# A two-layer SiLU block on one core: transposing two more blocks of x by DMA, and opening with two blocks and eight weight tiles

## The chip, the cores and the metric

The kernel runs on one core of a Trainium2 chip. The metric is the time of one execution on the device in microseconds (us), lower is better. It is given as the median of several runs, with the lowest and highest. The profile is of one execution; its span is about 1.5 us shorter than the time of the same execution. All points in time below are counted from the start of the span. A run is called fast or slow by its granted TensorE clock and its time; a difference under 2% is called "same".

## The reference

```python
B, S, D, F = 1, 2048, 640, 1728          # x [S,D], w1 [D,F], w2 [F,D], all bf16
h = jnp.einsum("bsd,df->bsf", x, w1)
h = silu(h)
out = jnp.einsum("bsf,fd->bsd", h, w2)
```

The first product needs x with its 640 columns on the partitions, so x must be transposed. The words used below:

- A **block** is 128 rows of x (16 of them). A **chunk** is four blocks, 512 rows. Chunk 0 is blocks 0 to 3.
- A **row block** k of w1 is its rows 128k to 128k+127 (five of them, k = 0 to 4). A **tile** ft is 128 columns of w1 (13 of them, and 64 columns left over).
- The **opening pass** is the part in which TensorE works through the row blocks in the order in which they land, and keeps the sums of several tiles open in PSUM, the memory into which TensorE writes.

## The kernel before

All loads are issued by SyncE (`sp`), in the order in which they are needed. The chunks 1 to 3 come transposed by DMA, behind all of w1. The four blocks of chunk 0 are loaded plainly and turned by TensorE.

```python
FA = 6
FG = [(6, 10), (10, FT)]
ld_x[0] = load(sp, x0[:, 0, :], x_v[:, 0, :])
ld_x[1] = load(sp, x0[:, 1, :], x_v[:, 1, :])
FH = 3
ld_k0a = load(sp, w1s[:, 0, 0:FH * P], w1_v[:, 0, 0:FH * P])
for k in range(DT):                       # row blocks of tiles 0 to 5
    lo = FH if k == 0 else 0
    ld_k.append(load(sp, w1s[:, k, lo * P:FA * P], w1_v[:, k, lo * P:FA * P]))
    if k in (1, 2):
        ld_x[k + 1] = load(sp, x0[:, k + 1, :], x_v[:, k + 1, :])
for a, b in FG:                           # tiles 6 to 9, then 10 to the end
    e = F if b == FT else b * P
    pt = load(sp, w1s[:, :, a * P:e], w1_v[:, :, a * P:e])
    ...
for c in range(1, NSC):                   # chunks 1 to 3, transposed by DMA
    for dt in range(DT):
        ld_xc[c] = tick(sp.dma_start_transpose(out=xT[:, dt, c * SCH:(c + 1) * SCH],
            in_=xf[c * SCH:(c + 1) * SCH, dt * P:(dt + 1) * P]), s, 16)
# ... w2 behind them
```

`turn(j, ...)` turns block j with five PE transposes into PSUM, and VectorE and ScalarE copy the result. The opening pass has four blocks and six tiles:

```python
k_pass(0, 0, 1, first=True, fts=range(FH)); ...   # blocks 0 and 1, row block 0
wait(pe, ld_k[1]);  k_pass(1, 0, 2)
t2 = turn(2, 7, 6)
wait(pe, ld_k[2]);  k_pass(2, 0, 2)
wait(pe, *t2)
for k in range(3):
    k_pass(k, 2, 3)                       # block 2 catches up
t3 = turn(3, 7, 6)
wait(pe, ld_k[3]);  k_pass(3, 0, 3)
wait(pe, *t3)
for k in range(4):
    k_pass(k, 3, 4)                       # block 3 catches up
wait(pe, ld_k[4]);  k_pass(4, 0, 4, last=True)
# then tiles 6 to 12 with all 512 columns of chunk 0, then chunks 1 to 3, then the second product
```

## Time and profile before

| | kernel before |
|---|---|
| time | 126.85 us (126.74 to 126.95, 3 runs) |
| TensorE busy | 122.8 of 125.1 us |
| TensorE waits for w1 | none |
| last Silu of chunk 0 starts | 19.82 us |

From the page of the kernel before, busy time and share of the span by engine (PE: TensorE's matmuls, PEld: its weight loads, DVE: VectorE, ACT: ScalarE, POOL: GpSimd; SP is SyncE, L207 is line 207 of the kernel):

```profile
PE 122.8 (98%) x652; PEld 59.0 (47%) x652; DVE 9.0 (7%) x16; ACT 39.9 (32%) x70; POOL 0.8 (1%) x7
```

From the waits of the kernel before (who waited <- for whom: us in total, times, longest), the entries of TensorE that have to do with data; there is none for w1:

```profile
PEld ps L207 <- DVE xT L183: 0.4, 2, 0.2
PEld ps L180 <- DMA x<-in_x_dram: 0.4, 1, 0.4
```

The chain of waits of the kernel before, in order of time from the opening pass on (start, length, what):

```profile
3.87 2.47 PE ps L207 x18
6.34 0.28 PE ps L180 x5
6.62 1.72 PE ps L207 x24
8.34 0.28 PE ps L180 x5
8.62 114.60 PE ps L207 x579
```

The two pieces of 0.28 us are the turns of blocks 2 and 3.

The DMA in that stretch, by microseconds (window and length, then busy time of each engine, granted clock, mean DMA share, GB/s):

```profile
7.00:8.00 1.00, 1.00 (x18) 0.86 (x16) 0.01 (x1) 0.03 (x1) 0.00 (x0) 1.00 0.91 304
8.00:9.00 1.00, 1.00 (x16) 0.81 (x13) 0.34 (x1) 0.34 (x1) 0.00 (x0) 1.00 0.93 309
9.00:10.00 1.00, 1.00 (x15) 0.81 (x14) 0.01 (x1) 0.03 (x1) 0.00 (x0) 1.00 1.06 353
```

Issues of the last two parts of w1 (KB, us from issue to landing):

```profile
w1s<-in_w_dram SPq DMA_DIRECT2D x1, 640.0 KB, 6.5
w1s<-in_w_dram SPq DMA_DIRECT2D x1, 560.0 KB, 7.6
```

They wait in the queue for long, and that harms nothing: the landing records put them at 11.3 and 12.9 us, and TensorE needs them at 12.0 and 16.3 us.

### The profile page before, as it was taken

To read this page: it belongs to the slowest core of one execution; us is meant where nothing else is said; L and a number is where in the kernel's file an instruction comes from. 1 tells how busy PE (TensorE), PEld (TensorE's weight loads), DVE (VectorE), ACT (ScalarE), POOL (GpSimd) and SP (SyncE) were. 2 spreads that over 40 slices of the span, in tenths; PEclk is the share of its full clock that TensorE was granted. 3 is DMA by queue.
4 is the path that set the end of the run, shared out by engine and by line. 5 is a ranking of instruction groups with operands and counts; after the bars stand their busy time and mean duration, and the time that the engine had idled before them with its cause. 6 is when DMAs were issued, how large, how long until landed. Compare 5 with 4: busy or idle time off the path is not lost.

```text
span 125.1 us, 1496 instructions
## 1 busy us (share of the span) xinstructions
PE 122.8 (98%) x652; PEld 59.0 (47%) x652; DVE 9.0 (7%) x16; ACT 39.9 (32%) x70; POOL 0.8 (1%) x7
## 2 busy tenths in 40 slices
PE   8999999999999999999999999999999999999993
PEld 6786444444444444444444443444444443444452
DVE  0220000000000000000000004202020210112021
ACT  4224955555555555555530003010101011010100
POOL 2000000000000000000000000000000000000000
PEclk9999999999999999999999999999999999999999
DMA  5899954446970000000000001441111111111112
GB/s 154 261 313 229 124 125 93 110 100 130 368 280 2 0 0 3 0 0 5 0 0 0 0 0 35 91 147 58 52 52 52 52 52 52 52 58 52 52 56 101
DMA packets 17398, 10.37 MB, mean 83 GB/s; under 512 B 10864, under 2 KB 17392, under 8 KB 17392
## 3 DMA queue, kind: packets, MB, share of 16 engines
q1 hardware_dynamic: 17248, 10.21, 31.2%
q8 instruction: 5, 0.08, 0.3%
q10 hardware_dynamic: 144, 0.07, 0.2%
q14 instruction: 1, 0.01, 0.0%
HBM read 5.16 MB, written 2.62 MB: 62 GB/s over the span
## 4 chain that ended last, share of the span: by engine, by line
PE 98%; ACT 0%; issue 0%; DVEq 0%
PE ps L207 95%; PE ps L171 2%; PE ps L180 1%; ACT o_sb L295 0%; DVEq L403 0%
## 5 line engine op out<-in xcount | busy, mean ns | idle before, releaser
L207 PE MATMUL ps<-xT,w1s 128*128 128x512 bf16 (+4 forms) x328 | 60.1, 353 | 0.0
L207 PE MATMUL ps<-w2s,hT 128*128 128x512 bf16 (+2 forms) x221 | 45.4, 367 | 0.0
L207 PEld LDWEIGHTS ps<-xT,w1s 128*128 128x128 bf16 (+1 forms) x328 | 29.5, 101 | 30.1 <-DVE xT L183 0.4
L211 ACT ACTIVATE hT<-ps 128x512 bf16<-128x512 f32 x52 | 30.3, 602 | 23.2 <-PE ps L207 23.2
L207 PEld LDWEIGHTS ps<-w2s,hT 128*128 128x128 bf16 x221 | 20.9, 98 | 24.5 <-issue 1.1
L295 ACT CAST o_sb<-ps 128x512 bf16<-128x512 f32 (+1 forms) x8 | 4.4, 545 | 42.2 <-PE ps L207 42.2
L207 PE MATMUL ps<-hT,w2s 128*128 128x512 bf16 x52 | 11.4, 379 | 0.0
L293 DVE CAST o_sb<-ps 128x512 bf16<-128x512 f32 (+1 forms) x9 | 6.1, 677 | 39.9 <-PE ps L207 39.9
L207 PEld LDWEIGHTS ps<-hT,w2s 128*128 128x128 bf16 x52 | 5.0, 98 | 6.3 <-issue 0.4
L293 DVE CAST oT<-ps 128x512 bf16<-128x512 f32 x2 | 1.3, 686 | 66.8 <-PE ps L207 66.8
L295 ACT CAST oT<-ps 128x512 bf16<-128x512 f32 x2 | 1.1, 588 | 11.1 <-PE ps L207 11.1
L191 ACT COPY xT<-ps 128x256 bf16<-128x256 bf16 x4 | 1.5, 372 | 5.3 <-PE ps L180 5.3
L171 PE MATMUL ps<-z 128*128 128x256 bf16 x10 | 2.5, 415 | 0.4 <-DVE z L124 0.4
L207 PE MATMUL ps<-w2t,hTt 64*128 64x512 bf16 (+2 forms) x17 | 2.2, 366 | 0.0
L180 PE MATMUL ps<-ident,x 128*128 128x128 bf16 x20 | 2.1, 264 | 0.0
L183 DVE COPY xT<-ps 128x384 bf16<-128x384 bf16 x4 | 1.4, 358 | 7.2 <-PE ps L180 7.2
L180 PEld LDWEIGHTS ps<-ident,x 128*128 128x128 bf16 x20 | 1.7, 119 | 0.4 <-DMA x<-in_x_dram 0.4
L171 PEld LDWEIGHTS ps<-z 128*128 128x128 bf16 x10 | 1.3, 140 | 0.9 <-DVE z L124 0.4
L211 ACT ACTIVATE hTt<-ps 128x512 bf16<-128x512 f32 x2 | 1.2, 597 | 1.1 <-PE ps L207 1.1
L150 ACT ACT_TABLE_LOAD x1 | 1.3, 1283 | 0.7 <-PEq L403 0.7
L207 PEld LDWEIGHTS ps<-w2t,hTt 64*128 64x128 bf16 x17 | 0.7, 94 | 1.4 <-issue 0.8
L207 PE MATMUL ps<-hTt,w2t 64*128 64x512 bf16 x4 | 0.6, 382 | 0.0
(10 smaller groups left out, 1.5 us busy)
## 6 DMA issues: line engine op xcount, KB each, us to landing
out_dram<-o_sb SPq DMA_DIRECT2D x15, 160.0 KB, 1.8
w2s<-in_w_dram SPq DMA_DIRECT2D x1, 1120.0 KB, 6.6
w2s<-in_w_dram SPq DMA_DIRECT2D x1, 960.0 KB, 8.8
w1s<-in_w_dram SPq DMA_DIRECT2D x4, 192.0 KB, 3.6
x<-in_x_dram SPq DMA_DIRECT2D x4, 160.0 KB, 2.5
w1s<-in_w_dram SPq DMA_DIRECT2D x1, 640.0 KB, 6.5
w1s<-in_w_dram SPq DMA_DIRECT2D x1, 560.0 KB, 7.6
xT<-in_x_dram SPq DMA_TRANSPOSE x15, 3.4
```

The source lines that it names most:

```text
L150: act.activation(out=warm[:, :], in_=warm[:, :], func=ACT.Silu)
L171: pe.matmul(ps[:, 3, 0:HB], lhsT=z[:, 0:P], rhs=z[:, :], start=True, stop=True)
L180: ins = pe.transpose(dst, x0[:, j, dt * P:(dt + 1) * P], ident[:, :])
L183: r = tick(dve.tensor_copy(out=xT[:, 0:nv, j * P:(j + 1) * P], in_=v[:, 0:nv * P].rearrange("p (k s) -> p k s", s=P),), s_dve)
L191: r = tick(act.copy(out=xT[:, nv:DT, j * P:(j + 1) * P], in_=a[:, 0:(DT - nv) * P].rearrange("p (k s) -> p k s", s=P),), s_act)
L207: return pe.matmul(o, lhsT=l, rhs=r, start=start, stop=stop, skip_group_check=shared)
L211: r = tick(act.activation(out=out_ap, in_=in_ap, func=ACT.Silu), s_act)
L293: r = tick(dve.tensor_copy(out=out_ap, in_=in_ap), s_dve)
L295: r = tick(act.copy(out=out_ap, in_=in_ap), s_act)
```

## The change

Its intent: the ten PE transposes of blocks 2 and 3 and their copies go away, the opening pass has a plain order, and SyncE gets to its transposes sooner because ScalarE (`act`) issues the rest of w1. The core of the diff:

```diff
-        FA = 6
-        FG = [(6, 10), (10, FT)]
+        FA = 8
+        FG = [(8, 11), (11, FT)]
@@ loads on SyncE @@
-            if k in (1, 2):
-                ld_x[k + 1] = load(sp, x0[:, k + 1, :], x_v[:, k + 1, :])
-        for a, b in FG:
-            ...
-            pt = load(sp, w1s[:, :, a * P:e], w1_v[:, :, a * P:e])
@@ transposes on SyncE: blocks 2 and 3 (256 rows) first @@
-        for c in range(1, NSC):
+        for c in range(NSC):
             s = sem(f"s_xc{c}")
+            t0_, t1_ = (HB if c == 0 else c * SCH), (c + 1) * SCH
             for dt in range(DT):
                 ld_xc[c] = tick(sp.dma_start_transpose(
-                    out=xT[:, dt, c * SCH:(c + 1) * SCH],
-                    in_=xf[c * SCH:(c + 1) * SCH, dt * P:(dt + 1) * P],
+                    out=xT[:, dt, t0_:t1_], in_=xf[t0_:t1_, dt * P:(dt + 1) * P],
                 ), s, 16)
@@ the rest of w1 on ScalarE @@
+        wait(act, ld_k[2])
+        for a, b in FG:
+            e = F if b == FT else b * P
+            pt = load(act, w1s[:, :, a * P:e], w1_v[:, :, a * P:e])
@@ opening: two blocks, eight tiles, two tiles to a PSUM bank @@
-        ... (turns of blocks 2 and 3, catching up)
+        for k in range(1, DT):
+            wait(pe, ld_k[k])
+            k_pass(k, 0, 2)
@@ chunk 0 in halves of 256 columns @@
+        for ft, m in [(8, 2), (10, 1), (11, 2)]:
+            wait(pe, ld_w1[ft])
+            half(ft, m, 0)
+        wait(pe, ld_xc[0])
+        for ft in range(0, FT, 2):
+            half(ft, min(2, FT - ft), HB)
```

More of the change, by code (lines that the diff above doesn't have):

```diff
@@ L132, in bass_standalone__dense_activation_silu__prompt_kernel @@
             ld_k.append(load(sp, w1s[:, k, lo * P:FA * P], w1_v[:, k, lo * P:FA * P]))
-            if k in (1, 2):
-                ld_x[k + 1] = load(sp, x0[:, k + 1, :], x_v[:, k + 1, :])
-        for a, b in FG:
-            e = F if b == FT else b * P
-            pt = load(sp, w1s[:, :, a * P:e], w1_v[:, :, a * P:e])
-            for ft in range(a, b):
-                ld_w1[ft] = pt
         barrier_wait_here(ET.SP)
@@ L213, in silu, with k_pass @@
             return r
-        def k_pass(k, j0, j1, first=False, last=False, fts=range(FA)):
+        wait(act, ld_k[2])
+        for a, b in FG:
+            e = F if b == FT else b * P
+            pt = load(act, w1s[:, :, a * P:e], w1_v[:, :, a * P:e])
+            for ft in range(a, b):
+                ld_w1[ft] = pt
+        def k_pass(k, j0, j1, first=False, fts=range(FA)):
             for ft in fts:
-                if first:
-                    wait(pe, bank_free[ft])
+                bk = ft // 2
+                h = (ft % 2) * HB
+                if first and ft % 2 == 0:
+                    wait(pe, bank_free[bk])
                 ins = mm(
-                    ps[:, ft, j0 * P:j1 * P],
+                    ps[:, bk, h + j0 * P:h + j1 * P],
                     w1s[:, k, ft * P:(ft + 1) * P],
                     xT[:, k, j0 * P:j1 * P],
-                    start=first, stop=(k == DT - 1), shared=True,
+                    start=(first and ft % 2 == 0), stop=(k == DT - 1), shared=True,
                 )
-                if last:
-                    silu(hT[:, ft, 0:SCH], ps[:, ft, :], ft, tick(ins, s_pe))
+                if k == DT - 1 and ft % 2 == 1:
+                    silu(
+                        hT[:, ft - 1:ft + 1, 0:HB],
+                        ps[:, bk, :].rearrange("p (m s) -> p m s", m=2),
+                        bk, tick(ins, s_pe),
+                    )
         wait(pe, *t0, ld_k0a)
@@ L234, in bass_standalone__dense_activation_silu__prompt_kernel @@
         k_pass(0, 1, 2, fts=range(FH, FA))
-        wait(pe, ld_k[1])
-        k_pass(1, 0, 2)
-        t2 = turn(2, 7, 6)
-        wait(pe, ld_k[2])
-        k_pass(2, 0, 2)
-        wait(pe, *t2)
-        for k in range(3):
-            k_pass(k, 2, 3)
-        t3 = turn(3, 7, 6)
-        wait(pe, ld_k[3])
-        k_pass(3, 0, 3)
-        wait(pe, *t3)
-        for k in range(4):
-            k_pass(k, 3, 4)
-        wait(pe, ld_k[4])
-        k_pass(4, 0, 4, last=True)
-        nxt = [FA]
+        for k in range(1, DT):
+            wait(pe, ld_k[k])
+            k_pass(k, 0, 2)
+        nxt = [FA // 2]
         def bank():
@@ L258, in bank, with half @@
             return b
-        for ft in range(FA, FT):
-            wait(pe, ld_w1[ft])
-            b = bank()
-            for k in range(DT):
-                ins = mm(ps[:, b, :], w1s[:, k, ft * P:(ft + 1) * P], xT[:, k, 0:SCH],
-                         start=(k == 0), stop=(k == DT - 1))
-            silu(hT[:, ft, 0:SCH], ps[:, b, :], b, tick(ins, s_pe))
+        def half(ft, m, c0):
+            b = bank()
+            for i in range(m):
+                for k in range(DT):
+                    ins = mm(
+                        ps[:, b, i * HB:(i + 1) * HB],
+                        w1s[:, k, (ft + i) * P:(ft + i + 1) * P],
+                        xT[:, k, c0:c0 + HB],
+                        start=(k == 0 and i == 0), stop=(k == DT - 1), shared=True,
+                    )
+            t = tick(ins, s_pe)
+            silu(hT[:, ft:ft + m, c0:c0 + HB],
+                 ps[:, b, 0:m * HB].rearrange("p (m s) -> p m s", m=m), b, t)
+        for ft, m in [(8, 2), (10, 1), (11, 2)]:
+            wait(pe, ld_w1[ft])
+            half(ft, m, 0)
+        wait(pe, ld_xc[0])
+        for ft in range(0, FT, 2):
+            half(ft, min(2, FT - ft), HB)
         for c in range(1, NSC):
```

## The prediction

> **What bounds it now.** TensorE. In the table of busy time its matmuls cover 122.8 of 125.1 us (98%), and the chain of waits is TensorE for 98% of the span, at full granted clock. The waits view shows TensorE idle some 0.4 us each for the zeroed tile, the first x block and the first xT copy; none for w1 or the transposed blocks. So only less TensorE work, or new idle time, can move the time.
>
> **What goes.** Ten PE transposes: the timeline has them in two groups of five, issued every 56 ns, 0.28 us a group: -0.56 us on the critical path. Their four copies (0.36 to 0.37 us) and two x loads (160 KB each) were hidden.
>
> **What is added to TensorE.** Next to nothing. Starts in the timeline lie 56 ns apart for 128 columns, 109.5 for 256, 162.5 for 384, 216 for 512; weight loads stay hidden, so a split costs about 2.5 ns. Chunk 0 goes from about 113 matmuls to about 138: +0.06 us. One more Silu (0.6 us) falls on an ACT that waits for PE anyway. TensorE: -0.5 us in all.
>
> **What moves.** The old opening had four blocks of work for six tiles of w1: tiles 6 to 9 landed at 11.2 us and were needed at 12.0; the rest landed at 12.8, needed at 16.3. The new opening has half the columns per tile, so it eats w1 about twice as fast: by the spacings, the five k passes end near 9.2 us, tiles 8 to 10 are needed then, tiles 11 and 12 near 10.9, and the DMA-transposed half of chunk 0 near 12.0. But the bytes to move by then are the same (2.87 MB: x and transposes 0.66, w1 2.21), which took until 12.8 us, and ScalarE issues its two loads only when row block 2 of w1 has landed, about 6.2 us (estimate from the landings before), so their data starts near 7 us.
> The DMA table shows x and w1 moving at 230 to 360 GB/s, but 80 to 280 where transposes met the last w1 load (10.5 to 12 us): transpose packets that normally take 18 ns took 1 to 2 us, until the slowest engine had finished its other load. Now this overlap is built in. The Trainium skill, "DMA: Bandwidth & Descriptors", section "Issuing engines are not separate DMA queues", says DMAs from different issuers run on the same 16 DMA engines and interleave, and that a second issuer saves only issue time; the trace shows issue at 0.47 us a load, so ScalarE saves little.
> Estimate: tiles 8 to 10 land at 9.5 to 10.5, 11 and 12 at 11 to 12.5, the transposed half at 12 to 14.5 us. TensorE therefore waits 0.5 to 2.5 us in total between 8 and 14 us. Blocks 4 to 7 are needed near 20 us and should land at 17 to 19.5; the rest is early enough.
>
> **Sum.** 126.85 - 0.5 + about 1.3 = 127.6 us; range 126.2 to 129.4. Chances: faster by over 2%: 0.01; within 2%: 0.90; slower by over 2%: 0.09.
>
> **What would show it.** Right: a new wait of TensorE for w1 or for xT from DMA between 8 and 14 us, 0.5 to 2.5 us; spacing of 256-column matmuls 109 to 110 ns; from 20 us on the two timelines are the same, shifted. Wrong: no such wait (then about 126.3 us); wider spacing of 256-column matmuls; or a wait for blocks 4 to 7.
>
> **What would make it wrong.** If the queues share well and the transposes run ahead of w1, the gain of 0.5 us shows. If transposes hold the engines back for longer than before, or a stall of several us drops TensorE's clock (its matmuls ran at half rate until 5.8 us), it is slower by over 2%.

## The result, and the profile after

The kernel after takes 127.66 us (127.30 to 127.77, 6 runs) against 126.87 us (126.73 to 127.45, 6 runs). The ratio is 1.0053, with a 95% interval of 1.0029 to 1.0076: slower by half a percent, within the 2% that count as the same. Ratios in this document are the mean time of one kernel's fast runs over that of the other's fast runs of the same rounds, so they are not quite the ratio of the quoted medians.

From the page of the kernel after, busy time by engine:

```profile
PE 121.5 (96%) x667; PEld 61.7 (49%) x667; DVE 8.3 (7%) x14; ACT 39.6 (31%) x69; POOL 0.8 (1%) x7
```

TensorE has 1.3 us less busy time in a span that is 1.1 us longer. From the waits of the kernel after, the entries that are new:

```profile
PEld ps L200 <- DMA w1s<-in_w_dram: 2.8, 3, 2.0
PE ps L200 <- DMA w1s<-in_w_dram: 2.4, 4, 1.7
```

Weight loads and matmuls waited for the same landings, so the two lines are to be read together, not added. The chain of waits of the kernel after, in order of time (only its end; SyncE's issues come before):

```profile
2.41 3.68 DMA w1s<-in_w_dram
6.09 0.02 issue
6.11 4.74 DMA w1s<-in_w_dram
10.85 0.05 issue
10.90 113.43 PE ps L200 x598
```

This chain is the whole story of the opening. SyncE's load of row block 2, issued at 2.41 us, lands at 6.09 us; only this releases ScalarE, which issues the load of tiles 8 to 10 at 6.11 us; that lands at 10.85 us, and only then does TensorE go on, without a break to the end. From the timeline of the kernel after:

```profile
4.58 0.56 PEld L200 LDWEIGHTS ps<-xT,w1s 128*128 128x128 bf16 x10 [0.41 <-DMA w1s<-in_w_dram]
5.54 3.39 PEld L200 LDWEIGHTS ps<-xT,w1s 128*128 128x128 bf16 x32 [0.40 <-DMA w1s<-in_w_dram]
6.11 1.14 ACTq L89 DMA_DIRECT2D w1s<-in_w_dram  x2
10.90 11.02 PEld L200 LDWEIGHTS ps<-xT,w1s 128*128 128x128 bf16 x97 [1.97 <-DMA w1s<-in_w_dram]
```

There are waits of 0.4 us for row blocks 0 and 1 (up to 4.58 and 5.54 us) and one of 1.97 us for tiles 8 to 10. The DMA by microseconds:

```profile
7.00:8.00 1.00, 1.00 (x12) 0.90 (x10) 0.00 (x0) 0.00 (x0) 0.00 (x0) 1.00 0.84 141
8.00:9.00 1.00, 1.00 (x12) 0.83 (x9) 0.00 (x0) 0.41 (x1) 0.00 (x0) 1.00 1.00 319
9.00:10.00 1.00, 0.21 (x2) 0.00 (x0) 0.00 (x0) 1.00 (x3) 0.00 (x0) 1.00 1.24 231
```

Between 7 and 8 us the rate falls to 141 GB/s, where the kernel before moved 304. SyncE's row blocks are through (the last landed at 7.47 us), and ScalarE's load, issued at 6.11 us, has its first packet at 7.4 us and its full rate only after 8 us. The engines were not idle in that microsecond (busy share 0.84): about half of the bytes were those of the first transposes, in small packets of 256 B. After 9 us the load is slowed a second time; e5 below comes back to that. The issues of ScalarE's loads:

```profile
w1s<-in_w_dram ACTq DMA_DIRECT2D x1, 480.0 KB, 4.7
w1s<-in_w_dram ACTq DMA_DIRECT2D x1, 400.0 KB, 5.7
```

**The account.** From the last Silu of chunk 0 to TensorE's end there are 103.4 us in both traces (19.82 to 123.20 and 20.94 to 124.32). So the whole difference of the two profiled runs, 1.12 us, arises in chunk 0. It splits as follows; each figure is a sum of distances between matmul starts in the two traces:

| term | us |
|---|---|
| two turns fewer (0.28 each), 25 matmuls more (2.5 ns each) | -0.50 |
| gaps beyond the usual spacing, from the first matmul of the opening pass (3.8 us) on: 0.23 before, 2.72 after | +2.49 |
| half-rate clock after 3.8 us: 0.91 before, 0 after | -0.91 |
| sum | +1.08 |
| measured | +1.12 |

The third term needs a word. At the start TensorE ran at half its rate: 213 ns from start to start for 256 columns, and later 109. In the profiled run of before this lasted until 5.8 us, in that of after until 3.1 us. The Trainium skill, "TensorE: Matmul & The Clock Gate", Part 1, says that the array starts at half rate, is released after a busy window of about 3.4 us, and that the window runs freely, so that the moment varies from run to run. These traces agree in the rates and in the variation; the spread here is larger than the 500 ns named there (3.1 to 6.5 us over the traces).

### The profile page after: what moved, and what is told of

It reads as the page before. It is cut to its first block, busy times and chain, and to the rows that moved or that the text cites. A ratio compares the mean times of both kernels' runs of the same rounds, so it can differ in the third digit from the quotient of the medians.

```text
span 126.2 us, 1523 instructions
## 1 busy us (share of the span) xinstructions
PE 121.5 (96%) x667; PEld 61.7 (49%) x667; DVE 8.3 (7%) x14; ACT 39.6 (31%) x69; POOL 0.8 (1%) x7
## 4 chain that ended last, share of the span: by engine, by line
PE 90%; DMA 7%; SPq 2%; issue 0%; ACT 0%
PE ps L200 90%; DMA w1s<-in_w_dram 7%; SPq L89 2%; ACT o_sb L301 0%; SPq L409 0%
## 5 line engine op out<-in xcount | busy, mean ns | idle before, releaser
L200 PE MATMUL ps<-xT,w1s 128*128 128x512 bf16 (+3 forms) x353 | 59.3, 335 | 2.4 <-DMA w1s<-in_w_dram 2.4
L200 PEld LDWEIGHTS ps<-xT,w1s 128*128 128x128 bf16 (+1 forms) x353 | 32.8, 98 | 28.6 <-DMA w1s<-in_w_dram 2.8
L204 ACT ACTIVATE hT<-ps 128x512 bf16<-128x512 f32 (+1 forms) x53 | 30.8, 589 | 29.0 <-PE ps L200 29.0
L173 PEld LDWEIGHTS ps<-ident,x 128*128 128x128 bf16 x10 | 0.9, 132 | 0.4 <-DMA x<-in_x_dram 0.4
L173 PE MATMUL ps<-ident,x 128*128 128x128 bf16 x10 | 1.1, 281 | 0.0
L184 ACT COPY xT<-ps 128x256 bf16<-128x256 bf16 x2 | 0.7, 372 | 0.9 <-PE ps L173 0.9
L176 DVE COPY xT<-ps 128x384 bf16<-128x384 bf16 x2 | 0.7, 358 | 2.8 <-PE ps L173 2.8
```

The source lines that it names most:

```text
L173: ins = pe.transpose(dst, x0[:, j, dt * P:(dt + 1) * P], ident[:, :])
L176: r = tick(dve.tensor_copy(out=xT[:, 0:nv, j * P:(j + 1) * P], in_=v[:, 0:nv * P].rearrange("p (k s) -> p k s", s=P),), s_dve)
L184: r = tick(act.copy(out=xT[:, nv:DT, j * P:(j + 1) * P], in_=a[:, 0:(DT - nv) * P].rearrange("p (k s) -> p k s", s=P),), s_act)
L200: return pe.matmul(o, lhsT=l, rhs=r, start=start, stop=stop, skip_group_check=shared)
L204: r = tick(act.activation(out=out_ap, in_=in_ap, func=ACT.Silu), s_act)
```

## The experiments

Each row is one kernel; the last column is read from the profiled run. The trace of one kernel is not that of the next execution: in the two traces of before, the same program, row block 2 landed at 6.29 and 6.90 us and row block 4 at 8.20 and 9.46 us. A difference of this size between two single traces is thus no proof of a cause.

| run | time, us | ratio to before, 95% | last Silu of chunk 0 |
|---|---|---|---|
| after | 127.66 | 1.0053 (1.0029 to 1.0076) | 20.94 |
| e1: ScalarE without its wait | 127.73 | 1.0052 (1.0028 to 1.0077) | 21.06 |
| e2: all w1 on SyncE, ahead of transposes | 128.81 | 1.0138 (1.0112 to 1.0163) | 22.24 |
| e3: no wait for tiles 8 to 12 (wrong result) | 127.32 | 1.0026 (0.9992 to 1.0060) | 20.36 |
| e4: before, with ScalarE's queue | 128.23 | 1.0096 (1.0067 to 1.0126) | 21.45 |
| e9: e2, blocks 2 and 3 turned by TensorE | 127.50 | 1.0039 (1.0016 to 1.0062) | 20.21 |
| e10: e4, transposes held | 127.92 | 1.0075 (1.0054 to 1.0096) | 21.12 |
| e6: after, one transpose for five | 129.55 | 1.0115 (1.0076 to 1.0154) | 23.64 (slow run; the two fast times are 128.01 and 128.82) |
| e7: e2, one transpose for five | 126.83 | 1.0001 (0.9964 to 1.0039) | 19.91 |
| before, again | 127.13 | 1.0004 (0.9983 to 1.0024) | 20.26 |
| e5: after, transposes held | 134.59 | 1.0591 (1.0534 to 1.0648) | 28.68 |
| e11: e7, row block 0 in one load | 126.55 | 0.9988 (0.9948 to 1.0028) | 19.40 |
| e12: e11, x block 1 issued by ScalarE | 125.95 | 0.9920 (0.9888 to 0.9952) | 18.61 |

All but e3 gave correct results. In the traces of e1 to e4, e9, e10, e6, e7 and e12 some ten matmul records are missing, so a gap is called a wait below only where the waits view names a releaser.

### e1: ScalarE's loads without their wait

```diff
-        wait(act, ld_k[2])
         for a, b in FG:
```

> ScalarE issues its two w1 loads without waiting for row block 2 (near 4 us instead of 6.1). Theory LATE (the 2 us wait of TensorE for tiles 8 to 10 comes from the late issue): they land about 2 us earlier, near 8.9 us, the wait shrinks from 2.0 to under 0.4 us, and part of the saving is eaten by the transposed half of chunk 0 (it landed at 13.0 us and would be needed at about 11.8): total about 126.8 us. Theory BLOCK (the wait comes from transposes that hold the DMA engines while the ScalarE loads run): tiles 8 to 10 still land at 10 us or later, and the time stays at 127.3 us or more.

Measured: 127.73 us, as the kernel after. From the waits of e1:

```profile
PEld ps L200 <- DMA w1s<-in_w_dram: 3.0, 6, 0.9
```

ScalarE issued at 3.59 us, 2.5 us earlier than in after, but tiles 8 to 10 landed at 10.67 us instead of 10.85. The two queues now shared the engines: row block 4 landed at 9.19 us instead of 7.47, and tiles 11 and 12 at 12.61 instead of 12.25. The one wait of 2.0 us became six of up to 0.9 us, with the same sum: 3.0 against 2.8 us. By the figures that I had written down this is the BLOCK outcome, but the waits say something simpler as well: taking the wait away let a later need compete with an earlier one. Both can hold: in e2, where the same loads stand ahead of the transposes in one queue, these tiles landed at 9.83 us.

### e2: all of w1 on SyncE's queue, ahead of the transposes

```diff
+        for a, b in FG:                   # right behind row block 4
+            ...
+            pt = load(sp, w1s[:, :, a * P:e], w1_v[:, :, a * P:e])
         ...
-        wait(act, ld_k[2])
-        for a, b in FG:
-            ... pt = load(act, ...)
```

> ScalarE's queue is not used: the same two w1 loads follow the five row blocks on SyncE's queue, ahead of all transposes. Both LATE and BLOCK: tiles 8 to 10 land near 8.3 us (1.64 MB had landed by 6.8 us in the kernel after, 0.49 MB more at about 330 GB/s), no wait for w1 at tile 8; tiles 11 and 12 near 9.5 us. The transposes start about 1 us later and the transposed half of chunk 0 lands near 13 us against a need at 11.8: a wait of about 1 us moves there. Total about 126.7 us, same as before. If the time is 126.0 or less, the transposed half came earlier than I think; if over 127.5, the transposes and not w1 are the bottleneck.

Measured: 128.81 us, slower than I expected by 2 us. Tiles 8 to 10 landed at 9.83 us, tiles 11 and 12 at 11.12 us, both a microsecond or more earlier than in after. But the wait moved. From the waits of e2:

```profile
PEld ps L205 <- DMA xT<-in_x_dram: 2.4, 1, 2.4
PEld ps L205 <- DMA w1s<-in_w_dram: 1.6, 3, 0.7
```

The last of the five transposes of blocks 2 and 3 landed at 14.89 us. Four of them took SyncE 1.24 us each to issue (the first 1.68), as long as one of 512 rows (1.26 us), so the fifth was not issued before 10.55 us. And of the 16 engines that carry it, 15 were done at 13.22 us and the last at 14.89; an instruction fetch of 16 KB was under way from 12.88 to 13.84 us. That the fetch held that engine is a guess from the times, not shown.

### e3: no wait for tiles 8 to 12 in the first half

```diff
-            wait(pe, ld_w1[ft])
-            half(ft, m, 0)
-        wait(pe, ld_xc[0])
+            half(ft, m, 0, ft - 8)        # weights of tiles 0 to 4: wrong result on purpose
+        wait(pe, ld_xc[0], ld_w1[8], ld_w1[11])
```

> Wrong result on purpose: the first-half tiles 8 to 12 use the weights of tiles 0 to 4, so nothing waits for ScalarE's loads until the second half. All DMAs are as in the kernel after. Theory ONE WAIT (the wait for tiles 8 to 10 is all that was lost): the time falls by its full 1.9 us, to about 125.7 us. Theory HIDDEN SECOND WAIT (the transposed half lands at 13.0 us and would be needed at 11.7 us without the first wait): TensorE waits about 1.2 to 1.4 us for xT from DMA and the time falls by only about 0.6 us, to about 127.0 us. I expect the second.

Measured: 127.32 us, 0.3 us less than after (the intervals of the two overlap), where the removed wait was 2.0 us. In the two profiled runs chunk 0 ends 0.6 us earlier than in after, as expected. From the waits of e3:

```profile
PEld ps L200 <- DMA w1s<-in_w_dram: 1.2, 2, 1.0
PEld ps L200 <- DMA xT<-in_x_dram: 0.6, 1, 0.6
```

The theory of one wait is out. In this run row block 1 landed 0.8 us later than in after (6.27 against 5.49 us), with nothing in the program ahead of it changed, and TensorE then waited for the transposed blocks, which landed at 13.0 us, as in after. Behind the wait at tile 8 stood the next one.

### e4: the kernel before with ScalarE's queue alone

```diff
-        for a, b in FG:
-            ... pt = load(sp, ...)
+        wait(act, ld_k[2])
+        for a, b in FG:
+            ... pt = load(act, ...)
```

> The kernel before with one part of the change: its last two w1 loads go from ScalarE's queue behind the same wait for row block 2; four blocks are still PE-transposed and the opening covers six tiles. Theory: the queue itself costs nothing, what hurts is that the new opening needs tile 8 at 9 us. Here tiles 6 to 9 are needed at 12.0 us; issued at 6.3 us they land at 11 to 12.5 us: no wait or under 0.5 us, 126.8 us plus 0 to 0.4. The rival (loads from ScalarE's queue beside transposes are slow by themselves) expects them at 13 us or later and 128 us.

Measured: 128.23 us, slower than before by 1%. I had expected no loss. The load of tiles 6 to 9 landed at 11.98 us, as expected, and no wait is put down to it. The loss came from elsewhere, and part of it is a flaw of the experiment. From the chain of waits of e4:

```profile
2.89 4.32 DMA w1s<-in_w_dram
7.23 0.43 ACTq L89
7.69 0.55 ACTq L89
8.28 0.38 ACT xT L186
8.80 1.17 PE ps L202 x18
```

ScalarE waits for row block 2 (until 7.21 us), issues its two loads for a microsecond, and only then copies its share of the turned block 2, for which TensorE waits. In the kernel after ScalarE has no turn to copy by then. An engine that works in order and is made to wait for a DMA delays all that stands behind the wait. The other part, a wait of 1.35 us for row block 2, is taken up by e10 and by the second profile of before.

### e9: no DMA transpose for chunk 0

All loads on SyncE as in e2; blocks 2 and 3 are loaded plainly behind tiles 8 to 10 and turned by TensorE after tile 10; transposes come behind all of w1.

```diff
+            if a == FA:
+                ld_x[2] = load(sp, x0[:, 2, :], x_v[:, 2, :])
+                ld_x[3] = load(sp, x0[:, 3, :], x_v[:, 3, :])
 ...
-        for c in range(NSC):
+        for c in range(1, NSC):
 ...
+            if ft == 11:
+                b = bank(); t2 = turn(2, b, b)
+                b = bank(); t3 = turn(3, b, b)
 ...
-        wait(pe, ld_xc[0])
+        wait(pe, *t2, *t3)
```

> The opening of the change (two blocks, eight tiles, halves), but with all loads on SyncE's queue and blocks 2 and 3 loaded plainly behind tiles 8 to 10 and turned by TensorE as in the kernel before; DMA transposes only for blocks 4 on, behind all w1 loads. Theory TRANSPOSES (DMA transposes in flight beside plain loads hold back all 16 engines, and the one of chunk 0 is late): tiles 8 to 10 land near 8.4 to 9.8 us, x blocks 2 and 3 before 11 us, waits of TensorE after 5 us together under 0.7 us; total 126.0 to 126.6 us, faster than before by 0.3 to 0.7%. Rival BYTES (the new opening needs its bytes sooner than the engines can move them, in whatever form): the waits between 5 and 14 us stay near 1.5 to 2 us and the total is 127.3 us or more.

Measured: 127.50 us. From the waits of e9:

```profile
PEld ps L208 <- DMA w1s<-in_w_dram: 1.4, 3, 0.6
```

The transposed half no longer matters (x landed at 10.0 and 10.4 us), and yet the kernel is slower than before. By total time the rival, BYTES, has it: the new opening order with everything on one plain queue still waits 1.4 us for w1, in three pieces. By the waits it does not: 0.6 of the 1.4 us lie before 5 us, and the 0.8 us after it are nearer to the mark of TRANSPOSES (under 0.7) than to that of BYTES (1.5 to 2). So this run does not decide between them; that the bytes force the wait in whatever form is ruled out by e12 below, where all of w1 lands in time. Tiles 8 to 10 landed at 9.56 us and were needed at 9.3.

### e10: e4 with the transposes held until row block 4 has landed

```diff
         ld_xc = {}
+        wait(sp, ld_k[4])
```

> The run with ScalarE's queue alone, with one wait added: SyncE holds its first DMA transpose until the last row block of w1 has landed. In that run TensorE waited 1.35 and 0.88 us for row blocks 2 and 3, and they landed 0.9 and 0.5 us later than in the kernel before. Theory TRANSPOSES: without transposes behind them the row blocks land as in the kernel before (2 near 6.3, 3 near 7.7, 4 near 8.2 us), these two waits fall below 0.6 us together, and the time falls from 128.2 to about 127.0 us. Rival (the clock of TensorE came up earlier there, and the waits only show what a slow clock had covered): the row blocks land no earlier and the time stays near 128.2 us.

Measured: 127.92 us. Row block 2 landed at 6.89 us (7.21 in e4, 6.29 in the first profile of before), and TensorE waited 1.1 us for it, though no transpose was in flight before 8.3 us. So this wait does not need the transposes. Row blocks 2, 3 and 4 did land 0.3 to 0.5 us earlier than in e4, but the two traces of before differ by more; the rival, the clock, is the better reading, not a shown one. The wait on ScalarE's copy was there as in e4 (0.9 us).

### The kernel before, profiled again

> The kernel before, unchanged, profiled once more: in its first profile TensorE ran at half rate until 5.9 us, in all other profiles of this study only until 3.2 to 4.4 us. Theory CLOCK (the slow start covered waits for w1): if the clock comes up near 3 to 4 us here, TensorE waits for row block 2 for about 0.3 to 0.6 us instead of not at all, and the Silu of chunk 0's last tile still starts within 0.5 us of 19.8 us. If it starts 0.8 us or more earlier, the early clock is a real gain and the first profile of before was an unlucky one. The times of this kernel (126.7 to 127.5 us in all runs so far) speak for the first.

Measured: 127.13 us, the same. From the timeline of this run:

```profile
4.23 1.44 PE L207 MATMUL ps<-xT,w1s 128*128 128x128 bf16 x15 [0.18 <-ACT xT L191]
5.73 0.45 PE L180 MATMUL ps<-ident,x 128*128 128x128 bf16 x5
6.95 0.28 PE L207 MATMUL ps<-xT,w1s 128*128 128x256 bf16 x1 [0.77 <-DMA w1s<-in_w_dram]
```

In the first profile the first 18 matmuls of the opening pass, the turn of block 2 and the start of row block 2 came at 3.77, 6.18 and 6.46 us, without a wait. Here the clock was up at about 3.4 us, TensorE was through with the turn of block 2 at 6.0 us, and waited 0.9 us for row block 2. Chunk 0 ended no earlier (20.26 against 19.82 us). So the kernel before, too, is bound in its first 7 us by how soon bytes land: a slow clock covers the wait, and a fast one shows it. Only part of the 0.9 us shows this, though: row block 2 landed at 6.90 us here and at 6.29 in the first profile, so 0.6 us of it are a later landing, and some 0.3 us are what the slow clock had covered. The -0.91 us in the account above is therefore not a gain of the change: with row block 2 at 6.29 us this run's chunk 0 would have ended at about 19.65 us (an estimate, 20.26 - 0.61), so the early clock would have won about 0.2 us, not 0.9. (This text of mine says that all other profiles came up by 4.4 us; e6, where matmuls ran at half rate until 6.5 us, is an exception that I had overlooked.)

### e6 and e7: one transpose in place of five

```diff
+            if c == 0:
+                ld_xc[c] = tick(sp.dma_start_transpose(out=xT[:, :, t0_:t1_], in_=xf[t0_:t1_, :]), s, 16)
+                continue
             for dt in range(DT):
```

e6 is after with this edit, e7 is e2 with this edit.

> The kernel after, with the five transposes of blocks 2 and 3 (1.24 us of issue each, 64 KB each) given as one transpose of 320 KB. Its data then runs ahead of ScalarE's w1 loads in one piece. Theory TRANSPOSES: it lands near 9 us, in its time ScalarE's loads stand still, tiles 8 to 10 land near 10.5 to 11.3 us, so the wait at tile 8 is still about 2 us, but nothing waits for chunk 0's second half: total 127.4 to 128.2 us. Theory BYTES gives the same sum; the run is to show whether one instruction can do the five and at what issue cost (estimate: 1.3 to 3 us).

> The run with all w1 loads ahead on SyncE's queue, with the five transposes of blocks 2 and 3 given as one. There the fifth transpose landed at 14.9 us because 1 of its 16 engines ended 1.7 us after the others, while an instruction fetch of 16 KB was under way, and TensorE waited 2.3 us. As one transpose behind the last w1 load (11.1 us there) it should land near 12.5 us, before that fetch: the wait shrinks to 0.5 us or less and the time to about 126.8 us. If the wait is due to the bytes of the transpose alone, it lands at 13.2 us or later and the time stays above 127.5 us.

One instruction does the work of five, with a correct result, and was issued in 1.35 us in e6 where five had taken 6.2. In e6 it landed at 9.76 us, tiles 8 to 10 at 11.89 us, 0.6 us later than expected, and TensorE waited 2.4 us for them. ScalarE's load, issued at 6.50 us, had its first packet only at 9.06 us, when most of the transpose had gone through: as theory TRANSPOSES said, the load stood still behind it. Two of e6's four runs were slow, the profiled one among them. There the granted clock fell to half at 13.3 us, shortly after that wait, for 3.4 us (a window of e6, columns as above; the granted clock, 0.55 in the mean, is the third number from the end):

```profile
13.00:16.00 3.00, 3.00 (x18) 2.16 (x17) 0.00 (x0) 0.98 (x2) 0.00 (x0) 0.55 1.36 179
```

That is a second cost that followed this wait: half of 3.4 us lost again, which matches the 1.5 to 2.4 us between e6's two fast runs and its two slow ones. One of e2's six runs (130.66 us against 128.6 to 129.0) has the same mean clock, 0.987. No run of the kernel after had it; why its wait of 2.0 us spared it is not shown.

e7 came out as expected: 126.83 us, equal to before. (The issue of its one transpose took 4.7 us: it stood behind 0.88 MB more of queued loads than in e6.) The transpose landed at 12.37 us and nothing waited for it; what was left were waits for w1 of 1.2 us in two pieces.

### e5: the kernel after with all transposes held until tiles 8 to 10 have landed

```diff
+        wait(sp, ld_w1[8])
         for c in range(NSC):              # moved behind ScalarE's loads in the program text
```

> The kernel after, with SyncE holding its first DMA transpose until ScalarE's load of tiles 8 to 10 has landed. To separate what made that load take 4.7 us from its issue at 6.1 us. Theory TRANSPOSES: nothing shares the engines with it but the last row block, so it lands at 9.2 us or earlier and the wait at tile 8 falls from 1.9 us to under 0.4 us. Theory LATE ISSUE: it still lands at 10.2 us or later. In either case the five transposes of chunk 0 (1.28 us of issue each, from about 9 us) land after 15 us, TensorE waits 3 us or more for them, and the total is 129 to 131 us.

This run was to settle what made ScalarE's load slow. Its issues, and its DMA between 7 and 10 us:

```profile
w1s<-in_w_dram ACTq DMA_DIRECT2D x1, 480.0 KB, 3.8
```

```profile
7.00:8.00 1.00, 1.00 (x11) 0.90 (x10) 0.00 (x0) 0.00 (x0) 0.00 (x0) 1.00 0.34 49
8.00:9.00 1.00, 1.00 (x12) 0.89 (x10) 0.00 (x0) 0.02 (x1) 0.00 (x0) 1.00 0.87 261
9.00:10.00 1.00, 0.60 (x6) 0.29 (x3) 0.00 (x0) 1.00 (x3) 0.00 (x0) 1.00 1.10 363
```

With not one transpose in flight the load, issued at 6.51 us, landed at 10.36 us: LATE ISSUE, by the mark of 10.2 us that I had set, but only just, and row block 2, which releases ScalarE, itself landed 0.4 us later here (6.49 us) than in after. Between 7 and 8 us the engines moved 49 GB/s, because SyncE's row blocks were through and ScalarE's load had not begun. ScalarE was let go by the landing of row block 2, and landing, issue and first packets together take longer than the two row blocks still queued. The transposes cost at least as much on top: from issue to landing the load took 3.8 us here and 4.7 us in after. The traces show where most of the 0.9 us went. From 9.5 to 10.5 us, with transposes in flight, the engines moved in after (half a microsecond a line)

```profile
9.50:10.00 0.50, 0.00 (x0) 0.00 (x0) 0.00 (x0) 0.50 (x2) 0.00 (x0) 1.00 1.40 151
10.00:10.50 0.50, 0.00 (x0) 0.00 (x0) 0.00 (x0) 0.50 (x2) 0.00 (x0) 1.00 1.16 118
```

at a busy share above 1, with the packets of ScalarE's load taking 108 ns in the mean; in e5 the same load moved at 359 and 360 GB/s there, with packets of 33 ns. Set beside e9 (one queue, no transposes ahead, these tiles at 9.56 us), this gives an estimate of the wait of 1.97 us, for which TensorE's weight loads stood idle from 8.93 us: 0.6 us until 9.56, which e9's plain order leaves too (e12 below removes them); 0.4 us for the late issue (6.11 + 3.85 = 9.96 us); 0.9 us for the transposes. Each comes from one trace, so the shares are not shown. Both causes are seen inside the trace of after, though: the gap between 7 and 8 us, and the slow stretch at 9.5 us, which e5 and e9, without those transposes, do not have. That the transposes made it is the nearest reading; how, no run shows.

The total was far above what I wrote, 134.6 us. TensorE waited 5.7 us for the transposed blocks, and then its clock was at half (windows of e5):

```profile
17.00:20.00 3.00, 1.27 (x7) 0.88 (x8) 0.00 (x0) 0.00 (x0) 0.00 (x0) 0.56 0.29 66
20.00:23.00 3.00, 3.00 (x16) 2.07 (x15) 0.00 (x0) 0.60 (x1) 0.00 (x0) 0.50 0.42 95
```

### e11 and e12: fewer and earlier issues at the start

e11 is e7 with row block 0 as one load. e12 is e11 with one x block issued by ScalarE at the very start, so that all of SyncE's later loads come one issue (0.47 us) earlier.

```diff
-        ld_k0a = load(sp, w1s[:, 0, 0:FH * P], w1_v[:, 0, 0:FH * P])
-            lo = FH if k == 0 else 0
+            lo = 0                        # e11: one load per row block
+        ld_k0a = ld_k[0]
```

```diff
-        ld_x[1] = load(sp, x0[:, 1, :], x_v[:, 1, :])
+        ld_x[1] = load(act, x0[:, 1, :], x_v[:, 1, :])     # e12
+        barrier_wait_here(ET.Activation)
```

> The best run so far (all w1 loads ahead on SyncE's queue, one transpose for blocks 2 and 3; 126.8 us) with the first row block of w1 as one load of 256 KB instead of 96 and 160 KB. Issue of all later loads moves 0.47 us earlier and their packets are 2 KB throughout. Expected if the opening is bound by how soon bytes arrive: row block 0 lands at about 4.1 us (TensorE starts 0.3 us later), row block 4 at about 7.7 and tiles 8 to 10 at about 9.2 us, each 0.5 us earlier than there, the wait at tile 8 falls from 0.67 to about 0.2 us: total 126.3 to 126.6 us. If the opening is bound by the engines' rate and not by issue, the later loads land no earlier and it costs 0.3 us: 127.1 us.

> The run with row block 0 as one load, in which TensorE's only wait left after 4 us was 1.48 us for that row block (issued third, at 1.0 us, landed at 4.78). Here ScalarE issues x block 1 at the start, beside SyncE, so that row block 0 is SyncE's second issue, near 0.55 us, and everything behind it follows 0.47 us earlier. Theory ISSUE (the head of the queue is bound by when loads are issued): row block 0 lands near 4.2 us, the wait falls to about 0.8 us, the rest stays without waits, the last Silu of chunk 0 starts near 18.9 us instead of 19.4 and the total is 125.7 to 126.0 us, which would beat both kernels by about 0.8%. Rival RATE (the engines moved 220 to 300 GB/s in the first 3 us and are the limit): row block 0 lands at 4.6 us or later, x block 0 later than 2.4 us, and the total stays near 126.5 us.

e11: 126.55 us, not separable from before. Its runs fall in two groups, 126.2 to 126.8 us and 127.6 to 127.8 us; why is open, since only one was profiled. The chain of waits of that one (126.19 us):

```profile
1.00 3.78 DMA w1s<-in_w_dram
...
4.92 117.88 PE ps L210 x646
```

Once row block 0 is there, TensorE runs to the end with no wait but 0.2 us at tile 8 (tiles 8 to 10 landed at 9.32 us, about as expected). Row block 0 itself landed at 4.78 us, 0.7 us later than expected. Only the start is left, and e12 goes at that. Its chain of waits:

```profile
0.09 2.43 DMA x<-in_x_dram
...
4.03 14.54 PE ps L211 x138
...
```

Row block 0, issued at 0.54 us, landed at 3.89 us instead of 4.78, x block 0 at 2.52 instead of 2.36. No wait for w1 is left, and chunk 0 ends at 18.6 us. The time is 125.95 us (125.39 to 126.32, 6 runs) against 127.11 us: ratio 0.9920, interval 0.9888 to 0.9952. By time and by row block 0, ISSUE has it; x block 0, later than 2.4 us, is the one sign of RATE. What ISSUE does not explain is the size: all of SyncE's later w1 loads landed 0.6 to 1.2 us earlier than in e11, for 0.47 us of issue saved. The kernel beats both others, the one before by about 0.8%: clear of noise, but still "same" by the rule of 2%. It keeps the new opening of the change and takes back the part in which ScalarE loads the rest of w1.

## Why the prediction was right or wrong

The forecast time, 127.6 us, and "within 2%" came out: 127.66 us. Point by point:

- **"Ten PE transposes: -0.56 us", "a split costs about 2.5 ns", TensorE -0.5 us in all: right.** The 256-column matmuls of the kernel after start 109 ns apart, and the account closes to 0.04 us with these figures.
- **A new wait of TensorE for w1 or xT between 8 and 14 us of 0.5 to 2.5 us: right in size.** It is 1.97 us. It stands at one place, tiles 8 to 10. I had spread it over tiles 8 to 10, tiles 11 and 12 and the transposed half; the last two landed in time (12.25 us against a need at 12.5, 13.0 us against 13.6), because the first wait had pushed their need back. e3 and e2 show that wait for the transposed half as soon as the first is taken away.
- **"Tiles 8 to 10 land at 9.5 to 10.5": missed by 0.35 us; they landed at 10.85.** The mechanism was there, and two terms of it were too small. The first is "so their data starts near 7 us": the first packet came at 7.4 us and the full rate after 8.0 us, because ScalarE was released by a landing, and between 7 and 8 us the engines moved 49 GB/s without transposes (e5) and 141 GB/s with them (after). The second is the overlap with transposes ("now this overlap is built in"): it cost 0.9 us if after and e5 are compared, and without it the load lands inside the forecast range (10.36 us in e5, and an estimated 9.96 us with the issue time of after). That the order of issue alone held the load, as the mark of e5 would have it, does not follow.
- **"DMAs from different issuers run on the same 16 DMA engines and interleave": right.** The Trainium skill, "DMA: Bandwidth & Descriptors", section "Issuing engines are not separate DMA queues", says so, and e1 shows it with numbers: when ScalarE issued 2.5 us earlier, its tiles landed 0.2 us earlier and row block 4 landed 1.7 us later. "ScalarE saves little" holds for the rest of w1. It need not hold for the first loads of the kernel: one issue saved on SyncE (0.47 us) gave 0.6 us by the medians (126.55 to 125.95 us) and 0.9 us by the ratios to before. By the two intervals anything from about 0.2 to 1.5 us is possible.
- **The waits before 8 us were missed.** I had none for row blocks 0 and 1; the kernel after waits 0.4 us for each. A row block is larger now (eight tiles, 256 KB, against six, 192 KB), and with two blocks of x in place of four it is used up sooner.
- **The clock was missed as well.** The prediction took the half rate until 5.8 us from the trace of before as given. It varies from run to run (3.1 to 6.5 us here). In the profiled pair it offsets 0.91 us of the new waits. That the sum of my terms (-0.5 + 1.3) hit the measured +0.8 so closely is in part luck: two omissions, more waits and an earlier clock, nearly cancel. The total is thus a weaker confirmation of the terms than it looks.
- **"Blocks 4 to 7 are needed near 20 us and should land at 17 to 19.5", "from 20 us on the two timelines are the same, shifted": right.** They landed at 19.3 us, were needed at 20.7, and the rest of both traces is 103.4 us long.

What stays open: the exact shares of late issue and transposes in the landing at 10.85 us, since a single trace of each was taken, and how the transposes slowed the load's packets; why e12 gained more than its issue time; the cause of the one late engine under the transposes (e2); and the two groups of times in e11.

## What to carry to other kernels

Where a start is bound by bytes, keep the loads in one queue in the order of need: a second issuer that runs freely takes rate from earlier needs (e1), and one that waits for a landing leaves the engines with little to do between that landing and its own first packet (1.1 us in e5). Removing one wait is worth only the distance to the next one, so look at what lands second and third before expecting the whole gain (e3: 2.0 us of wait removed, 0.3 to 0.6 us won). Count DMA instructions as well as bytes: five transposes of 64 KB cost SyncE 6.2 us, one of 320 KB cost 1.35 us where the queue ahead of it was short (4.7 us where it was long), and a single issue moved off the busy queue at the very start was worth about 0.6 us here.

## What the Trainium skill lacked or had wrong

- "DMA: Bandwidth & Descriptors" gives no issue time of a DMA transpose measured on trn2. Here it is 1.24 us for 256 rows by 128 columns and 1.26 us for 512 by 128, so it hardly depends on the rows, and 1.35 us for 256 by 640 in one instruction with three dimensions at the destination (e6; 4.7 us behind a longer queue, e7). That one instruction can turn several column blocks into a destination of three dimensions is not said there either.
- "Advanced Engine Details and Errata", section "X-Bar Transpose (TRN2)", says that transposes are as fast as regular DMAs and expects 350 to 400 GB/s. Here the one transpose of 320 KB, alone on the engines, moved at 282 GB/s (e6, 8.5 to 9 us), against 363 for plain loads (e5, 9 to 10 us); separate ones with nothing else in the queues are bound by their issue, 128 KB every 1.30 us, 100 GB/s.
- "DMA: Bandwidth & Descriptors", section "Issuing engines are not separate DMA queues", says that issuing from several engines saves only issue time, "usually small relative to the DMA itself". It does not say that at the start of a kernel this time can stand on the critical path: one load moved to ScalarE was worth about 0.6 of 126.6 us (e11 to e12), with the reservations above.
- No page says that gating a second issuer on a landing leaves a hole in the DMA traffic: 49 GB/s for 1 us in e5, where a single queue moved 304 GB/s at the same time.
- No page says that a plain load that is followed in its queue by transposes lands on all 16 engines almost at once: within 0.07 us for row block 4 of after and 0.16 us for the last w1 load of before, where SyncE's other w1 loads of 192 to 640 KB in these two traces spread over 0.8 to 2.3 us (ScalarE's two over 0.6 and 0.2 us). The cause was not tested.
- "TensorE: Matmul & The Clock Gate", Part 1, gives ±500 ns for the moment at which the clock comes up. By the spacing of the matmuls it came between 3.1 and 6.5 us in the traces. Its warning that idle TensorE falls back to half rate is borne out: a granted clock of one half for 6.8 us that began within a wait of 5.7 us (e5), and half rate for 3.4 us that began 1.3 us after a wait of 2.4 us (e6, a slow run). The second wait is shorter than the window of 3.4 us that the page gives.
- The same Part 1 warns that clock events in traces can be unreliable, but does not say that they fail at the start of a kernel: the granted clock reads full speed throughout in the profile of before, while matmuls of 256 columns were 213 ns apart until 5.8 us.
